# One weight tile cut by partitions, and w_ch moved behind it

## The chip, the cores and the metric
The kernel runs on one core of a Trainium2 chip. The metric is device time in microseconds (us): the median of several runs. Beside it there is one profiled execution, whose span (first to last instruction) and trace are read here. TensorE (PE) multiplies, VectorE (DVE) and ScalarE (ACT) work element by element, GpSimd (POOL) here mostly issues transfers, SyncE (SP) issues the stores and the first loads.

## The reference, cut to what matters
Attention with a forgetting decay, then a spectral mix of 64 Fourier modes along the sequence, then a residual channel product:

```python
# q, k, v: 8 x 8 heads x 576 x 64; f: 8 x 8 x 576
scores = q @ k.T / 8 + (cum[i] - cum[j])        # cum: running sum of log f; causal
x = softmax(scores) @ v                         # put together as 8 x 576 x 512
X = rfft(x, axis=1)[:, :64]                     # 64 modes of 512 channels
Yr = Xr @ w_r - Xi @ w_i                        # w_r, w_i: 64 x 512 x 512, one matrix a mode
Yi = Xr @ w_i + Xi @ w_r
u = x + irfft(Y)
out = u + relu(u @ w_ch)                        # w_ch: 512 x 512
```

The inputs are float32 in HBM; w_r and w_i are 67 MB each, and every weight is used once. w_ch is 1 MB.

## The kernel before
**Two stages.** The first runs over 32 pairs of heads (plus two iterations to drain): transposes of q and k, scores, exponentials, the product with v, and the Fourier sums of each finished pair. From its iteration 10 on, `spec_early` also multiplies the first channel blocks with their weights. The second stage runs over the 16 groups `u` of four modes and, in each, over the channel blocks `dc` still missing; between them `xw` and `fold` multiply by w_ch and bring the modes back to the sequence. After the last weight come 18 steps that add up and store the result.

**The weights.** `wseq` lists the weight tiles in the order of use: first the 28 of `early`, (u, 0) for 16 groups and (u, 1) for 12; then for each u what is left. A tile with `dc < 2` holds w_r and w_i of four modes for 128 channels and comes as two transfers (L156), which `issue_half` sends one at a time. A tile with `dc` 2 or 3 holds w_r or w_i of four modes for 256 channels, two channels on each partition, and comes as one transfer of 128 partitions (L165): 2 MB read from HBM as float32, 1 MB written as bfloat16. The first tile of that kind is number 28, `n == len(early)`; it is sent by the `issue_half` of iteration 29 of the first stage. The very last tile of `wseq` comes mode by mode in four transfers. Tiles lie in seven buffers of `wpool` and, for five of them, in memory that is not yet in use (`guests`).

**The queue.** All weights, q, k, and v but for its first three, are issued by GpSimd, in the order in which the program is written: in each iteration q and k of the pair four ahead (L109), half a tile, v of the pair three ahead (L119), another half (left out in iterations 3, 6, 9, 12 and 15). An issue waits until its buffer is free, and until the transfer eight before it on this queue is complete (eight semaphores are used in turn). The transfers convert float32 to bfloat16 on the way (v excepted).

**w_ch.** `setup_late`, called once in iteration 2, loads all of w_ch in one transfer of 128 partitions (L322): 1 MB read, 0.5 MB written. On each partition lie four rows, the blocks `eb` 0 to 3. Its first reader is `xw` (L694) in the second stage; `fold_modes` (L718) and `last_modes` (L893) read it later.

**The end.** For the last group, `spec_cols` (L211) takes the last tile mode by mode as its four transfers land; then `last_modes`, `rest`, `base` and the stores follow (L953).

Of the kernel before, what the change touches and what calls it, by code (L numbers as in the profile page):

```python
# [17 lines left out]
def _strided(ap: bass.AP, free_dims, offset_elems: int = 0) -> bass.AP:  # L18
    new_ap = [list(ap.ap[0])] + [list(x) for x in free_dims]
    return bass.AP(tensor=ap.tensor, offset=ap.offset + offset_elems, ap=new_ap)  # L20
# [3 lines left out]
def kernel(  # L24
# [11 lines left out]
    nc = tc.nc  # L36
# [32 lines left out]
    wch = const.tile([128, NEB, D], BF16, name="wch")  # L69
# [55 lines left out]
    early = [(u, 0) for u in range(NU)] + [(u, 1) for u in range(NX)]  # L125
# [14 lines left out]
    def issue_w(half=None):  # L140
        n = wissued[0]
        if n >= len(wseq):
            return
        u, dc = wseq[n]
        if half != 1:
            if n in guests:
                w8 = guests[n][:, 0 : 8 * D].rearrange("p (t m e) -> p t m e", t=2, m=4)
            else:
                shape = [128, 2, 4, D] if dc < 2 else [128, 4, 2, D]
                w8 = wpool.tile(shape, BF16, tag="w8", name="w8")  # L150
            wtile[(u, dc)] = w8
        w8 = wtile[(u, dc)]
        if dc < 2:
            for t, src in enumerate((moe_w_r, moe_w_i)):
                if half in (None, t):
                    nc.gpsimd.dma_start(  # L156
                        w8[:, t, :, :],
                        src[4 * u : 4 * u + 4, dc * 128 : (dc + 1) * 128, :].rearrange("m p e -> p m e"),
                    )
        elif half != 1:  # L160
            src = (moe_w_r, moe_w_i)[dc - 2]
            step = 1 if n + 1 == len(wseq) else 4
            for j in range(0, 4, step):
                m = 4 * u + j
                nc.gpsimd.dma_start(  # L165
                    w8[:, j : j + step, :, :].rearrange("p m r e -> p m (r e)"),
                    src[m : m + step, 256:512, :].rearrange("m (p r) e -> p m (r e)", r=2),
                )
        if half != 0:
            wissued[0] += 1  # L170

# [2 lines left out]
    def issue_half():  # L174
        issue_w(whalf[0])
        whalf[0] ^= 1
# [138 lines left out]
    def setup_late():  # L315
        nc.vector.memset(XS[:, :, 24 * NM : XROW], 0.0)
        nc.vector.tensor_copy(
            perm[:].rearrange("p (b j ri) -> p b j ri", b=8, j=4),
            ident_bf[:].rearrange("p (j x ri b) -> p b j x ri", j=4, x=2, ri=2)[:, :, :, 0, :],
        )  # L320
        nc.vector.tensor_copy(rep[:], _strided(ident_bf[:, KF:128], [[0, 4], [1, KL]]))
        nc.gpsimd.dma_start(wch[:], moe_w_ch.rearrange("(eb p) e -> p eb e", p=128))  # L322

    def setup_bi(sc):
        ns = SBLK[sc]
# [226 lines left out]
    for i in range(NPAIR + 2):  # L552
# [56 lines left out]
        if i == 2:  # L609
            setup_late()  # L610
# [12 lines left out]
    with ExitStack() as bctx:  # L623
# [44 lines left out]
        with ExitStack() as mctx:  # L668
# [97 lines left out]
            for u in range(NU):  # L766
# [4 lines left out]
                for dc in range(first, NEB):  # L771
# [37 lines left out]
                    else:  # L809
                        spec_mms(A, u, dc, dc == first, dc == NEB - 1)  # L810
                    issue_w()
                if last:
                    break
# [103 lines left out]
        for i in range(len(steps)):  # L917
# [11 lines left out]
            p, sb = steps[i][0]  # L929
# [54 lines left out]
```

## Time and profile before

| | |
|---|---|
| median of 3 runs | 436.59 us (436.33 to 437.64) |
| profiled execution | 436.43 us, span 434.6 us |
| busy: PE, DVE, ACT, POOL | 343.3, 267.9, 234.1, 145.0 us |
| read from HBM, written | 163.73 MB, 9.44 MB |
| GpSimd's transfers (q0) | 62800 packets, 85.64 MB |

Busy times are sums over an engine's instructions. Bytes of a queue are counted as written, so a weight counts half of what is read for it. "q8" and "q14" are the queues that carry instructions, q1 that of SyncE's loads and stores. A transfer is done in sixteen shares; the trace keeps the time at which each is complete. Rows of a timeline give start, duration, engine, line, operation and, in brackets, the idle time before and what ended it; rows of the chain that ended last give start, duration and what. All times count from the span's start.

### The profile page before, as it was taken

What the parts mean: (1) busy time and instruction counts of PE and PEld (TensorE: products, weight loads), DVE (VectorE), ACT (ScalarE), POOL (GpSimd) and SP (SyncE); (2) the same over time, 40 slices, a digit from 0 to 9 for tenths busy, and PEclk for the clock granted to TensorE, in tenths of its full rate; (3) what the DMA queues carried; (4) which work ended last, traced back from release to release, by engine and by line L of the source; (5) the groups of instructions that cost most, each with busy time, mean ns of one, the idle gap of its engine ahead of it and who ended that gap; (6) DMA issues with size and microseconds to landing.
All of it is one profiled execution on the core that took longest, in us unless ns stands there. A gap on an engine that the chain in (4) does not pass through costs nothing.

```text
span 434.6 us, 10304 instructions
## 1 busy us (share of the span) xinstructions
PE 343.3 (79%) x4264; PEld 189.6 (44%) x4274; DVE 267.9 (62%) x651; ACT 234.1 (54%) x358; POOL 145.0 (33%) x215
## 2 busy tenths in 40 slices
PE   1689787798898898988896386599877498888993
PEld 1455555554555565555553142244433233334330
DVE  6677888877778778888885122222233165565794
ACT  4556777687887766656660022024322166564783
POOL 6544445444544353444213211111122202110273
PEclk9986999999999999999999579589999699999998
DMA  8999999999999999999999999999999999998498
GB/s 185 205 233 220 233 219 232 225 227 233 231 229 227 226 228 225 228 225 228 227 218 213 212 212 211 212 212 213 211 212 212 209 209 211 210 209 158 168 383 323
DMA packets 68543, 96.76 MB, mean 223 GB/s; under 512 B 3728, under 2 KB 45200, under 8 KB 68496
## 3 DMA queue, kind: packets, MB, share of 16 engines
q0 software_dynamic: 62800, 85.64, 106.3%
q1 hardware_dynamic: 5696, 10.47, 6.6%
q8 instruction: 33, 0.54, 0.4%
q14 instruction: 14, 0.11, 0.1%
HBM read 163.73 MB, written 9.44 MB: 398 GB/s over the span
## 4 chain that ended last, share of the span: by engine, by line
DMA 43%; PE 31%; DVE 18%; issue 3%; ACT 3%; POOL 1%; DVEq 0%; POOLq 0%
DMA w<-in_moe_w_r_dram 22%; DMA w<-in_moe_w_i_dram 20%; PE pav L477 5%; DVE vT L384 4%; DVE qkT L360 4%; DVE x_all L492 4%; PE A L194 4%; PE sps L432 3%; PE tv L382 3%; PE pd L521 3%; PE vp L393 2%; DMA qk<-in_k_dram 2%; PE Z L654 2%; DVE vn L372 2%; PE U L654 2%
## 5 line engine op out<-in xcount | busy, mean ns | idle before, releaser
L439 ACT ACTIVATE et<-sps 128x1024 bf16<-128x1024 f32 x96 | 96.0, 1049 | 13.9 <-PE sps L432 11.5
L477 PE MATMUL pav<-vs,et 128*128 128x65 bf16 (+1 forms) x896 | 52.1, 198 | 0.2 <-DVE vn L372 0.2
L360 DVE COPY qkT<-tp 128x640 bf16<-128x640 bf16 x64 | 48.7, 763 | 2.8 <-PE tp L355 2.8
L815 DVE TENSOR_TENSOR Yb<-A,yx 128x512 bf16<-128x512 f32 x15 | 10.4, 691 | 61.0 <-PE A L194 60.9
L477 PEld LDWEIGHTS <-et 128*128 128x128 bf16 (+1 forms) x896 | 37.2, 103 | 17.9 <-issue 13.6
L432 PE MATMUL sps<-qkT 64*128 64x512 bf16 (+4 forms) x320 | 39.8, 312 | 1.1 <-DVE qkT L360 1.1
L194 PE MATMUL A<-w,XP 128*16 128x512 bf16 (+1 forms) x240 | 21.9, 449 | 23.0 <-DMA w<-in_moe_w_i_dram 12.8
L694 PE MATMUL pxw<-wch,xT 128*128 128x512 bf16 (+1 forms) x152 | 39.0, 402 | 0.9 <-issue 0.3
L492 DVE TENSOR_TENSOR x_all<-pav,rcp 128x384 bf16<-128x384 f32 (+2 forms) x96 | 36.2, 377 | 3.3
L355 PE MATMUL tp<-ident_bf,qk 128*64 128x128 bf16 x576 | 30.3, 237 | 9.3 <-DMA qk<-in_k_dram 9.3
L384 DVE COPY vT<-tv 128x576 bf16<-128x576 bf16 x32 | 24.2, 757 | 19.8 <-PE tv L382 19.8
L165 POOL DMA_DIRECT2D w<-in_moe_w_r_dram x16 | 11.9, 743 | 71.8 <-PE A L194 50.5
L701 ACT CAST XW<-pxw 128x512 bf16<-128x512 f32 (+1 forms) x16 | 9.4, 585 | 47.3 <-PE pxw L694 47.3
L156 POOL DMA_DIRECT2D w<-in_moe_w_r_dram x27 | 20.5, 758 | 38.7 <-DMA w<-in_moe_w_i_dram 9.4
L404 ACT COPY vs<-vp 128x576 bf16<-128x576 bf16 x32 | 20.5, 640 | 21.7 <-PE vp L400 21.7
L165 POOL DMA_DIRECT2D w<-in_moe_w_i_dram x19 | 13.3, 698 | 53.3 <-PE A L194 31.6
L701 ACT CAST yx<-pxw 128x512 bf16<-128x512 f32 (+1 forms) x24 | 14.0, 585 | 31.4 <-PE pxw L694 31.4
L109 POOL DMA_DIRECT2D qk<-in_q_dram x32 | 19.5, 610 | 32.5 <-PE sps L432 6.2
L741 ACT CAST x_all<-pu 128x512 bf16<-128x512 f32 (+1 forms) x40 | 23.4, 584 | 11.2 <-PE pu L740 10.3
L491 DVE RECIPROCAL rcp<-pav 128x6 f32<-128x6 f32 (+2 forms) x96 | 16.2, 169 | 17.4 <-PE pav L477 17.3
L156 POOL DMA_DIRECT2D w<-in_moe_w_i_dram x27 | 20.3, 752 | 18.4 <-DMA w<-in_moe_w_i_dram 8.2
L109 POOL DMA_DIRECT2D qk<-in_k_dram x32 | 19.2, 601 | 19.3 <-DMA w<-in_moe_w_i_dram 5.2
(149 smaller groups left out, 677.8 us busy)
## 6 DMA issues: line engine op xcount, KB each, us to landing
w<-in_moe_w_r_dram POOLq DMA_DIRECT2D x16, 1024.0 KB, 29.5
w<-in_moe_w_i_dram POOLq DMA_DIRECT2D x15, 1024.0 KB, 31.7
w<-in_moe_w_r_dram POOLq DMA_DIRECT2D x27, 512.0 KB, 11.1
w<-in_moe_w_i_dram POOLq DMA_DIRECT2D x27, 512.0 KB, 12.3
out_dram<-o_sb SPq DMA_DIRECT2D x36, 256.0 KB, 3.2
vt<-in_v_dram POOLq DMA_DIRECT2D x29, 288.0 KB, 10.7
qk<-in_q_dram POOLq DMA_DIRECT2D x32, 144.0 KB, 10.8
qk<-in_k_dram POOLq DMA_DIRECT2D x32, 144.0 KB, 10.4
```

The costliest lines, as they stand in the source:

```text
L109: nc.gpsimd.dma_start(qk[64 * n : 64 * n + 64, :, :], src[b, 2 * g : 2 * g + 2, :, :].rearrange("h (p r) d -> p h (r d)", p=64),)
L156: nc.gpsimd.dma_start(w8[:, t, :, :], src[4 * u : 4 * u + 4, dc * 128 : (dc + 1) * 128, :].rearrange("m p e -> p m e"),)
L165: nc.gpsimd.dma_start(w8[:, j : j + step, :, :].rearrange("p m r e -> p m (r e)"), src[m : m + step, 256:512, :].rearrange("m (p r) e -> p ...
L194: nc.tensor.matmul(A[32 * j : 32 * j + M, :], lhsT=lhsT, rhs=rhs, start=st_, stop=sp_)
L355: nc.tensor.transpose(tp[64 * hp : 64 * hp + 64, r - r0, :, :].rearrange("p n c -> p (n c)"), qk[:, hp, r * 64 : r * 64 + 64], ident_bf[:, :],
L360: nc.vector.tensor_copy(st[i]["T"][:].rearrange("p n (c r) -> p n c r", r=9)[:, :, :, r0:r1], tp[:, 0 : r1 - r0, :, :].rearrange("p r n c ...
L384: nc.vector.tensor_copy(st[i]["vT"][:].rearrange("p (c r) -> p c r", r=9), tv[:].rearrange("p r c -> p c r"))
L432: nc.tensor.matmul(ps[:, hp, c : c + n], lhsT=KT[sl, jb * 128 : jb * 128 + 128], rhs=QT[sl, i0 : i0 + n], start=True, stop=True,)
L439: nc.scalar.activation(st[i]["et"][:, T, :, :], ps[:], ACT.Exp, scale=scale)
L477: nc.tensor.matmul(pav[:Ms, sb % 3, hp, :], lhsT=eblk(i, hp, jb, sb), rhs=rhs, start=(jb == 0), stop=(jb == sb),)
L492: nc.vector.tensor_tensor(x_all[:ns, g, b, lo:hi, :].rearrange("p s (h d) -> p s h d", h=2), pav[:ns, lo % 3 : lo % 3 + n, :, 0:Dh], _stri ...
L694: nc.tensor.matmul(pxw[rows, :], lhsT=xT[:, eb, sb * 128 : sb * 128 + Ms], rhs=wch[:, eb, :], start=(eb == 0), stop=(eb == NEB - 1),)
```

## The change
The first tile of the second kind, number 28, is loaded in three transfers, of partitions 0 to 14, 15 to 63 and 64 to 127 (15, 49 and 64 of them), in place of one of 128. Right behind it, in the same `issue_w`, w_ch is loaded in three: its blocks 0 and 1 in partitions 0 to 71 and 72 to 127 (72 and 56), then its blocks 2 and 3 in all 128. The load in `setup_late` is gone.

```diff
             step = 1 if n + 1 == len(wseq) else 4
+            cuts = (0, 15, 64, 128) if n == len(early) else (0, 128)
             for j in range(0, 4, step):
                 m = 4 * u + j
-                nc.gpsimd.dma_start(
-                    w8[:, j : j + step, :, :].rearrange("p m r e -> p m (r e)"),
-                    src[m : m + step, 256:512, :].rearrange("m (p r) e -> p m (r e)", r=2),
-                )
+                rows = src[m : m + step, 256:512, :].rearrange("m (p r) e -> p m (r e)", r=2)
+                for p0, p1 in zip(cuts, cuts[1:]):
+                    nc.gpsimd.dma_start(
+                        w8[p0:p1, j : j + step, :, :].rearrange("p m r e -> p m (r e)"), rows[p0:p1]
+                    )
+            if n == len(early):
+                rows = moe_w_ch.rearrange("(eb p) e -> p eb e", p=128)
+                for p0, p1, e0 in ((0, 72, 0), (72, 128, 0), (0, 128, 2)):
+                    nc.gpsimd.dma_start(wch[p0:p1, e0 : e0 + 2, :], rows[p0:p1, e0 : e0 + 2, :])
...
         nc.vector.tensor_copy(rep[:], _strided(ident_bf[:, KF:128], [[0, 4], [1, KL]]))
-        nc.gpsimd.dma_start(wch[:], moe_w_ch.rearrange("(eb p) e -> p eb e", p=128))
```

Every byte that was loaded is still loaded once, on the same queue.

## The prediction

> **What bounds the kernel now.** I read the page first: the DMA row, the queues and the chain that ended last.
>
> ```profile
> span 434.6 us, 10304 instructions
> ...
> DMA  8999999999999999999999999999999999998498
> ...
> q0 software_dynamic: 62800, 85.64, 106.3%
> ...
> q8 instruction: 33, 0.54, 0.4%
> ...
> DMA 43%; PE 31%; DVE 18%; issue 3%; ACT 3%; POOL 1%; DVEq 0%; POOLq 0%
> ```
>
> The transfer engines are busy in every slice but the last few, and the transfers that GpSimd issues (q0) carry nearly all of it. Next, the chain in order of time, in the last 100 us, shows where the stream hands over to the tail:
>
> ```profile
> 352.85 29.27 DMA w<-in_moe_w_r_dram
> 382.12 0.28 issue
> 382.40 19.71 DMA w<-in_moe_w_i_dram
> 402.12 0.05 issue
> 402.16 0.41 PE AT L211 x8
> ...
> 428.65 0.60 DVE o_sb L938
> ```
>
> The last weight piece lands at 402.12. What follows is arithmetic and stores, 32.5 us to the end of the span, and none of it is touched. So the question is what moves 402.12.
>
> The trace keeps sixteen completion marks for each transfer, one for each transfer engine, without the engine's number. For the last piece, sorted, in us behind the first (396.61):
>
> ```
> 0.00 0.55 0.63 0.87 0.88 1.50 1.70 | 3.58 4.59 4.62 4.89 4.96 5.22 5.25 5.27 5.51
> ```
>
> Seven engines are early, nine late, and the kernel waits for the last. The offsets are not one transfer's accident: from 214 us to the end each 1 MB weight transfer passes all sixteen at the same 4.95 us pace (first marks at 217.73, 222.68, 227.64), and the offsets stay, apart from single steps of about 1.06 us on one engine at a time. The steps go with the packets of q8: 33 of 16 KB, each taking 0.89 to 1.03 us. The first starts at 23.35, and the transfer landing then has its last mark at 25.39, 1.06 behind the next to last (24.32), where the one before it had 0.03 there. Their durations repeat in turns of eight (949, 945, 935, 974 ns open the first turn, 949, 944, 935, 974 the fourth), so I read them as eight engines served in rotation. By 396 us 32 of them have run, four for each of eight engines: 4 x 1.06 = 4.24, plus the spread of 0 to 1.04 that all had at 18 us. That is the group at 4.59 to 5.51; the 3.58 is then an engine hit by the smaller fetches of q14. When an early engine has finished (396.61) the others do not speed up: the last four pieces still come 1.25 apart. Each engine has its own pace, so work taken off a late engine comes off the end, and work put on an early one costs nothing until it is the last.
>
> **The change part by part.** It moves no arithmetic: the instructions of TensorE, VectorE and ScalarE stand in the same order, so the q8 fetches stay 33.
>
> *w_ch out of the setup (L322).* Its half megabyte passed an engine in 2.54 us (first marks 41.21 and 43.75). Everything behind it on GpSimd's queue comes up to 2.54 us earlier until the tile that brings it back. The sum over the span is nothing as long as no engine runs dry: GpSimd's issues in the attention follow the completion of the transfer eight before (0.28 to 0.6 us after it nearly always), so the depth stays. Where buffers hold GpSimd instead (78.27 and 148.47, some 1.5 us late), the queue could lose 2.54 of a depth (issue to first mark) of 7.82 and 6.35, leaving 5.28 and 3.81; the very first transfer, into an empty queue, took 3.27. Covered, by 0.5 us at the worst. If that cover were gone it would cost the early engines alone, up to 2.5. w_ch's first reader is L694 at 252.0 us, and it now lands near 230: 20 us to spare.
>
> *One tile in three transfers, w_ch in three.* The tile is the first of L165; GpSimd's rows are
>
> ```profile
> 210.23 0.74 POOL L165 DMA_DIRECT2D w<-in_moe_w_r_dram  x1 [0.31 <-issue]
> 211.05 0.74 POOL L165 DMA_DIRECT2D w<-in_moe_w_i_dram  x1
> 217.54 0.74 POOL L165 DMA_DIRECT2D w<-in_moe_w_r_dram  x1 [5.75 <-PE tv L382]
> ```
>
> Six issues replace one here: five more at 0.55 to 0.74 us, 3.3 us of GpSimd, hidden by the 5.75 it idles. They also use up the eight places in flight: the next tile's issue (211.05) now waits for the mark that stood at 219.68, less 2.54, so about 217.2. Behind it wait only the further tiles; the early engines pass the tile ahead at 217.73 - 2.54 = 215.2 and then have 12 rows (7.4 us) and some 2 us of w_ch, the late ones start 3 us later with 5 rows and 3 us of w_ch: work until about 224. A transfer needs some 3 us, so it is covered by 4. Five more transfers cost each engine something: quarter tiles pass in 1.25 to 1.27 against 4.95 / 4 = 1.24, so 0.02 each, 0.10 in all.
> [...]
>
> *Who carries the rows.* 64 and 128 partitions cost all sixteen engines alike. No row of before shows 15, 49, 72 or 56. A row of the tile costs an engine 4.95 / 8 = 0.62 us, a row of half of w_ch 2.54 / 16 = 0.16. Bounds: spread evenly, nothing changes; given to few engines, some gain rows and others lose them. I take equal shares over the largest number of engines up to sixteen that divides the count, because a transfer in equal shares is what every row shows: 15 as 15x1, 49 as 7x7, 64 as 16x4, 72 as 12x6, 56 as 14x4, each going on where the one before stopped. Counting engines from where the 15 starts as 0: the 49 lies on 15 and 0 to 5, the 72 on 6 to 15, 0 and 1, the 56 on 2 to 15. (15+7+12+14 is 48, so the turn closes.) Against 8 rows each:
> - 0 and 1: tile 1+7+4 = 12, w_ch 6: +4 x 0.62 - 2 x 0.16 = +2.16
> - 2 to 5: 12 and 4: +2.48 - 0.64 = +1.84
> - 15: 0+7+4 = 11 and 10: +1.86 + 0.32 = +2.17
> - 6 to 14: 1+4 = 5 and 10: -1.86 + 0.32 = -1.54
>
> Seven engines get more, nine less, and the trace has seven early and nine late. If these are the same, the late end at 5.51 - 1.54 = 3.97 and the early at most at 1.70 + 2.17 = 3.87: the gap closes almost exactly. That fit of numbers and of sizes is why I take this placement, though no row names an engine.
> [...]
>
> *Sum.* -1.54 + 0.10 = -1.44 us on 402.12. TensorE must follow:
>
> ```profile
> 341.88 1.06 PE L194 MATMUL A<-w,XP 128*16 128x512 bf16 x8 [4.25 <-DMA w<-in_moe_w_i_dram]
> 371.86 0.64 PE L194 MATMUL A<-w,XP 128*16 128x512 bf16 x8 [0.81 <-DMA w<-in_moe_w_i_dram]
> 402.16 0.40 PE L211 MATMUL AT<-XP,w 128*128 128x16 bf16 x8 [0.31 <-DMA w<-in_moe_w_i_dram]
> ```
>
> It waits 4.25 us for a tile at 341.88, so its work from there starts 1.44 earlier too, and the later, small waits move with it. Span 434.6 - 1.44 = 433.16; the profiled execution's 436.43 lies 1.83 above its span, which gives 434.99. The median of the runs shown, 436.59, is 0.16 above that execution: 435.15, say 435.1.
>
> **The rivals.**
> 1. *The seven heavy shares meet late engines* (slower). Decided by where the turn stands: one engine of the 4.59 to 5.51 group among the heavy seven is enough. It ends at up to 5.51 + 2.17 = 7.68 instead of 5.51: 436.59 + 2.17 + 0.10 = 438.9. For it: the trace names no engine. Against it: seven and nine match, and so do the prices. Chance 0.15.
> 2. *Shares rounded up over sixteen*: 15 as one each on fifteen, 49 as four on twelve and one on a thirteenth, 72 as five, 56 as four. Twelve engines then carry 9 and 9 rows: +0.62 + 0.16 = 0.78; four lose. With nine late engines, at least five of the twelve are late: 4.96 to 5.51 + 0.78 + 0.10, so +0.3 to +0.9, 436.9 to 437.5. [...] Chance 0.12.
> 3. *TensorE does not follow.* Between 341.88 and 402.16 its waits for weights are 0.3 to 0.8 each, and it ran at half clock near 340 to 350 (0.43 us a matmul against 0.22). If that stretch does not move with the landings, only the last waits are won: 0.3 to 0.8, so 435.8 to 436.3. Chance 0.05.
> 4. *Nothing uneven happens* (the transfers spread over all sixteen whatever their count): +0.1, 436.7. Chance 0.04.
>
> The forecast keeps 0.64.
>
> **How the numbers follow.** 0.3% is 1.31 us, about what a measurement of this kernel can tell from no change. The forecast's 1.44 is just over it, so of its 0.64 I give 0.56 to faster and 0.08 to falling short of the bound. Same: that 0.08 with rivals 2, 3 and 4 (0.12, 0.05, 0.04), 0.29. Slower: rival 1, 0.15. The best that any division could do is level all sixteen at their mean, 3.13, which saves 2.38: 434.2; with the scatter of the runs, 434.0 is the low end. The high end, 437.5, takes in rival 2 and leaves out rival 1.
>
> **What would show it.** In the profile after, the sixteen marks of the last piece should lie within 4 us, with last near 400.7 and the first near 398.5, and the marks of the 49-partition transfer should bunch: seven engines busy 4.3 us, nine passing at once. w_ch's first reader should wait for nothing, and GpSimd's issue of the next tile should stand near 217. Wrong would be: a last mark over 403 with a spread of 7 (rival 1), a spread near 6 (rival 2), or an earlier landing with an unmoved end (rival 3).

## The result: 438.02 us, slower by a quarter of a per cent

The changed kernel takes 438.02 us (22 runs, 437.13 to 439.64), the kernel before 437.0 in the same comparison (22 runs, 436.02 to 438.0): ratio 1.0026, 95% interval 1.0016 to 1.0035. That is 1.1 us by the ratio and 1.0 by the medians, inside the 0.3% that the prediction took as its bound but clear over 22 runs of each. It is on the other side of no change from the forecast (435.1), and past the high end of its range (437.5). The profiled execution took 437.98 us.

The page of the changed kernel, in the rows shown of before, has the same stream and a span 1.6 us longer:

```profile
span 436.2 us, 10319 instructions
...
DMA  8999999999999999999999999999999999997498
...
q0 software_dynamic: 63184, 85.64, 106.3%
...
q8 instruction: 33, 0.54, 0.5%
...
DMA 42%; PE 34%; DVE 17%; ACT 3%; issue 3%; POOL 1%; DVEq 0%; POOLq 0%; ACTq 0%
```

The bytes are the same to the last figure, the instruction fetches (q8) are 33 as before. The sixteen marks of the last piece, in us behind the first (395.75; before 396.61), are

```
0.00 0.32 3.48 3.72 3.75 4.14 4.67 4.86 4.88 4.94 4.97 5.07 5.42 5.79 6.96 8.20
```

The first engine is done 0.86 earlier than before and the last 1.83 later, at 403.95 instead of 402.12. Before, seven engines were early and nine late. Now two are far ahead, two far behind, and the rest lie together. TensorE's rows at the same three places (start, duration, engine, line, and the idle time before with what ended it) are

```profile
342.91 1.06 PE L200 MATMUL A<-w,XP 128*16 128x512 bf16 x8 [4.21 <-DMA w<-in_moe_w_i_dram]
372.88 1.06 PE L200 MATMUL A<-w,XP 128*16 128x512 bf16 x8 [1.84 <-DMA w<-in_moe_w_i_dram]
404.00 0.40 PE L217 MATMUL AT<-XP,w 128*128 128x16 bf16 x8
```

The three stand 1.03, 1.02 and 1.84 later than before. The last has no wait behind it: TensorE gets there 0.05 after the last mark, so stream and TensorE end together in this run. The chain that ended last accordingly runs over the weights to 372.84 and then over TensorE:

```profile
309.24 33.63 DMA w<-in_moe_w_i_dram
342.91 0.49 issue
343.40 29.44 DMA w<-in_moe_w_i_dram
...
404.00 0.42 PE AT L217 x8
...
430.48 0.60 DVE o_sb L943
```

The clock granted to TensorE in that stretch was 0.89 where it was 1.00 before. The windows (busy time of PE, PEld, DVE, ACT, POOL with instruction counts, then granted clock, DMA share and GB/s) of before and then after:

```profile
372.00:402.00 30.00, 26.23 (x226) 11.84 (x221) 16.69 (x28) 15.94 (x28) 3.35 (x8) 1.00 1.05 192
```

```profile
372.00:402.00 30.00, 26.57 (x204) 11.86 (x203) 15.99 (x27) 15.53 (x28) 3.34 (x8) 0.89 1.07 194
```

In eight of the eleven profiled runs compared in the next sections (all but those of the probes), the time is the last mark plus 34.0 to 34.5 us (before 436.43 - 402.12 = 34.31, after 34.03). In the other three (e1_move, e2_cut, e10_fit) it is 35.2 to 35.4, and there TensorE reached the last piece 1.1 to 1.2 us after the mark, with 0.89 granted in the same window in all three. So the last mark sets the time, and in these three single runs the low clock went with some 1 us more; in the changed kernel, with the same 0.89, the late mark covers it (34.03). A last mark by itself scatters: that of e1_move stands at 403.15, 1.03 behind that of before, with no uneven share in it and with timed runs that agree with those of before. So a last mark is read below together with the pattern of the sixteen and with the timed runs.

GpSimd's rows after show the issues in their new order:

```profile
207.70 1.34 POOL L168 DMA_DIRECT2D w<-in_moe_w_r_dram  x2 [0.44 <-PE s L428]
210.46 0.62 POOL L168 DMA_DIRECT2D w<-in_moe_w_r_dram  x1 [1.42 <-DMA w<-in_moe_w_r_dram]
211.21 0.68 POOL L174 DMA_DIRECT2D wch<-in_moe_w_ch_dram  x1
213.73 0.63 POOL L174 DMA_DIRECT2D wch<-in_moe_w_ch_dram  x1 [1.84 <-DMA w<-in_moe_w_i_dram]
216.31 0.71 POOL L174 DMA_DIRECT2D wch<-in_moe_w_ch_dram  x1 [1.96 <-DMA w<-in_moe_w_r_dram]
217.86 0.76 POOL L168 DMA_DIRECT2D w<-in_moe_w_i_dram  x1 [0.83 <-PE sps L437]
```

Pieces of 15 and 49 go out together, then the 64, then w_ch in three, and the next tile at 217.86. The marks of the 49-partition piece, behind its first at 215.84, show the cut at work:

```
0.00 0.07 2.49 4.08 4.17 4.18 4.31 4.38 4.47 4.54 4.98 5.08 5.09 6.50 8.15 8.64
```

### The profile page after: what moved, and what is told of

Same layout as the page of the kernel before. It is cut to its first block, busy times and chain, and to the rows that moved or that the text cites. A ratio compares the mean times of both kernels' runs of the same rounds, so it can differ in the third digit from the quotient of the medians.

```text
span 436.2 us, 10319 instructions
## 1 busy us (share of the span) xinstructions
PE 347.5 (80%) x4274; PEld 191.2 (44%) x4274; DVE 268.3 (61%) x651; ACT 234.1 (54%) x358; POOL 147.5 (34%) x219
## 4 chain that ended last, share of the span: by engine, by line
DMA 42%; PE 34%; DVE 17%; ACT 3%; issue 3%; POOL 1%; DVEq 0%; POOLq 0%; ACTq 0%
DMA w<-in_moe_w_i_dram 28%; DMA w<-in_moe_w_r_dram 12%; PE pav L482 5%; DVE vT L389 4%; DVE x_all L497 4%; DVE qkT L365 4%; PE A L200 4%; PE sps L437 3%; PE tv L387 3%; PE vp L398 2%; PE pd L526 2%; DMA qk<-in_k_dram 2%; PE Z L659 2%; PE U L659 2%; DVE vn L377 2%
## 5 line engine op out<-in xcount | busy, mean ns | idle before, releaser
L168 POOL DMA_DIRECT2D w<-in_moe_w_r_dram x18 | 13.1, 727 | 68.7 <-PE A L200 36.9
L156 POOL DMA_DIRECT2D w<-in_moe_w_r_dram x27 | 20.5, 759 | 41.7 <-PE A L200 8.8
L689 DVE COPY xT<-ptr 128x576 bf16<-128x576 bf16 x32 | 14.6, 457 | 19.2 <-PE ptr L684 18.3
```

The source lines that it names most:

```text
L156: nc.gpsimd.dma_start(w8[:, t, :, :], src[4 * u : 4 * u + 4, dc * 128 : (dc + 1) * 128, :].rearrange("m p e -> p m e"),)
L168: nc.gpsimd.dma_start(w8[p0:p1, j : j + step, :, :].rearrange("p m r e -> p m (r e)"), rows[p0:p1])
```

## Experiments

**The theories.** A: the division is as forecast (equal shares over the largest divisor, in turn), but the heavy shares fall on engines of the late group. B: the heavy engines are the early ones, and the loss comes from elsewhere: from w_ch's new place, from five more transfers, or from a queue that runs empty. C: the division itself is another. The first three kernels do one part of the change each.

**e1_move: w_ch moved, nothing cut.** The tile is whole, w_ch comes whole behind it.

```diff
-            cuts = (0, 15, 64, 128) if n == len(early) else (0, 128)
+            cuts = (0, 128)
-                for p0, p1, e0 in ((0, 72, 0), (72, 128, 0), (0, 128, 2)):
-                    nc.gpsimd.dma_start(wch[p0:p1, e0 : e0 + 2, :], rows[p0:p1, e0 : e0 + 2, :])
+                nc.gpsimd.dma_start(wch[:], rows)
```

Expected:

> w_ch comes in one transfer of 128 partitions behind tile 28, which stays whole. Theory P (placement: the loss of 1.0 us comes from heavy shares that meet late engines): no uneven share is left, so equal to the kernel before within 0.3 us, last piece complete with the same spread of about 5.5 us. Theory M (the move itself lets an engine run dry or comes too late): the 1.0 us stays. Theory C (every added transfer costs): one transfer as before, so no change.

Measured: 436.92 against 436.97, ratio 0.9994 (0.9978 to 1.001); the last piece's marks run from 397.04 over 6.11 us, to 403.15, with seven early and nine late, as before. The move costs nothing that the timed runs can tell; the last mark of this one execution is the late one named above.

**e2_cut: the tile cut in 15, 49 and 64, w_ch left in the setup.**

```diff
+            cuts = (0, 15, 64, 128) if n == len(early) else (0, 128)
...
+                for p0, p1 in zip(cuts, cuts[1:]):
```

Expected:

> The tile in 15, 49 and 64 partitions, w_ch whole in the setup as before. Theory P: the seven heavy shares stay (+4 or +3 rows of 0.62 us), so slower by 0.7 to 2.5 us, and the sixteen marks of the last piece spread over about 8 us. Theory M: equal to before. Theory C: two transfers more, +0.2 us at most, with a spread of 5.5 us.

Measured: 438.47 against 436.97, ratio 1.0032 (1.0017 to 1.0046). The last piece's marks, behind 394.99:

```
0.00 0.88 4.13 4.22 4.34 4.48 4.54 4.69 4.97 5.08 5.39 5.40 5.72 6.45 6.86 8.62
```

The pattern of the changed kernel is there with the cut of the tile alone: two ahead, one alone at the end, last mark 403.61. The cut is what costs.

**e3_even: as many transfers, but in even shares.** 16, 48 and 64 partitions, and w_ch in 64, 64 and 128.

```diff
-            cuts = (0, 15, 64, 128) if n == len(early) else (0, 128)
+            cuts = (0, 16, 64, 128) if n == len(early) else (0, 128)
-                for p0, p1, e0 in ((0, 72, 0), (72, 128, 0), (0, 128, 2)):
+                for p0, p1, e0 in ((0, 64, 0), (64, 128, 0), (0, 128, 2)):
```

Expected:

> As many transfers in the same places as in the changed kernel, but in 16, 48 and 64 partitions, and w_ch in 64, 64 and 128: all of these divide evenly over sixteen engines. Theory P: equal to before within 0.3 us, spread 5.5 us. Theory C (five more transfers cost each engine 0.1 to 0.5 us): slower by 0.1 to 0.5 us with the spread of before. Theory M: slower by about 1 us.

Measured: 437.39 against 436.97, ratio 1.001 (0.9993 to 1.0027); last mark 402.25, 0.13 from before. From the tile ahead of the cut to the tile behind w_ch an average engine needs 12.63 us, in e1_move 12.56: the added transfers cost an engine 0.07. The interval alone (up to 0.27%) would leave room for the loss of the changed kernel, but the marks keep the pattern of before, seven early and nine late over 5.65 us, where those of e2_cut, with fewer transfers, do not. So the count of transfers is not the cause; the unevenness is.

**e4_probe: which engine is which?** Eight transfers of two rows from one place in HBM to another (in `out`, ahead of its stores), one behind every second large tile.

> The kernel before with eight more transfers of two rows (16 KB read each) in the second stage, one behind every second weight tile; they put other rows into a part of out that is stored later. A look at the sixteen marks: if a transfer of two partitions goes to two neighbouring engines and the next one goes on behind them (the division in equal shares with a turning start), each probe delays two of the sixteen marks by 0.6 us or more, and the eight together each pair once, so that the late and the early engines can be told by their place in the turn. If the late nine are neighbours in the turn, the first theory of placement stands; if late and early alternate, no block of seven fits.

A miss: 438.02 in one run (before 436.97), and no mark stepped away from the others, so they told no engine from another.

**e5_probe17: sixteen transfers of 17 partitions x 512 into a tile.** 17 is a prime, so by the forecast's division one engine would take all of it.

```diff
+                nc.gpsimd.dma_start(
+                    XS[17 * r : 17 * r + 17, 0, 512 * c : 512 * c + 512],
+                    moe_w_r[0, 256:290, :].rearrange("(p r) e -> p r e", r=2)[:, 0, :],
+                )
```

> The kernel before with sixteen more transfers of 17 partitions (2 KB read on each, into memory that is no longer in use), one behind each of sixteen successive weight tiles of the second stage. 17 has no divisor up to sixteen but 1. Theory P (equal shares over a divisor, the next transfer going on behind the last): each one falls on a single engine and delays one of the sixteen marks by 17 x 0.08 = 1.3 us, and the sixteen together go once round the engines, so the order in which late and early marks move is the order of the engines in the turn. With the placement that the prediction took, counted from the turn's start, the marks of 0 to 5 and 15 are early ones and those of 6 to 14 late ones; if late engines lie among 15 and 0 to 5, that is the error. Rounded-up shares: nine marks move by 0.16 us each time.

439.16 in one run (before 436.13). No engine took all. Nine marks, the same nine each time, fell behind by 0.16 (eight of them) or 0.07 (one) with each probe; the seven others kept their pace. By these times that is a share rounded up, two rows on eight engines (0.16), one on a ninth (0.07), none on seven, and it starts at the same engine each time. Numbered from there, and as the next probe numbers them, the two rows lie on engines 0 to 7 and the one on 8. Of engines 0 to 7 five marks are early, one lies in the middle and two are late; engine 8 is early; of 9 to 15 one is early and six are late. So the early seven are not one run of neighbours, as the forecast had them. In this two-dimensional form, then, 17 partitions were divided as rival 2 had it.

**e6_probe17x2: the same with a third dimension.** Two blocks of 256 in place of one of 512, the shape of a weight tile.

```diff
-                    XS[17 * r : 17 * r + 17, 0, 512 * c : 512 * c + 512],
-                    moe_w_r[0, 256:290, :].rearrange("(p r) e -> p r e", r=2)[:, 0, :],
+                    XS[17 * r : 17 * r + 17, 0, 512 * c : 512 * c + 512].rearrange("p (m e) -> p m e", m=2),
+                    moe_w_r[0:2, 256:273, 0:256].rearrange("m p e -> p m e"),
```

> The same sixteen small transfers of 17 partitions, but each partition's 2 KB now in two pieces from two matrices (17 x 2 x 256 elements), a shape in three dimensions as the tile's (49 x 4 x 1024) and w_ch's (72 x 2 x 512) are; in two dimensions (17 x 512) the shares were rounded up over nine engines, always the same nine. If three dimensions are shared by a divisor from a turning start, each transfer now delays one mark by 1.3 us, a different one each time, and the marks of heavy and light engines in the changed kernel follow from that order. If three dimensions are rounded up as well, nine marks move 0.16 each time, and the changed kernel's 1.0 us must come from twelve engines with one row more.

442.14 in one run (before 436.86). Now each probe holds up a single mark by 1.22 us, another one each time, and after sixteen each has had its turn. The marks of the tile ahead of the first probe (behind 267.13), of the first and of the second probe (behind 267.31 and 272.48):

```
0.00 0.21 0.32 0.34 0.78 1.12 1.36 2.58 3.15 3.25 3.39 4.00 4.77 5.74 5.81 5.95
0.00 0.25 0.34 0.82 1.17 1.38 1.56 2.61 3.15 3.29 3.41 3.99 4.78 5.75 5.82 5.94
0.00 0.23 0.33 0.81 1.36 1.54 2.37 2.60 3.15 3.28 3.40 3.98 4.77 5.74 5.80 5.93
```

At the first one of the marks near 0.34 goes to 1.56: engine 0. At the second 1.13 goes to 2.37: engine 1. Followed through all sixteen, and read at the last piece, where every engine has had one probe, the lags are

```
engine  8    7    15   0    4    1    2    3    9    5    6    14   13   11   12   10
lag   0.00 0.22 0.32 0.34 0.80 1.15 1.71 3.11 4.25 4.35 4.47 5.11 5.75 5.87 5.95 6.89
```

(15 and 0 are a pair that can't be told apart by 0.02.) The early seven are 0, 1, 2, 4, 7, 8 and 15; 3 lies between; 5, 6 and 9 to 14 are late. The heavy seven of the cut, 15 and 0 to 5, hold five early engines, the middle one and a late one, number 5; the early engines 7 and 8 were relieved instead. Theory A holds. The division by the largest divisor in turn, which the forecast took, agrees with these rows: 17 partitions held up one mark by 1.22 us at each probe, and sixteen probes sixteen different ones.

**The order as a lever: four kernels in two pairs.** If the engines are known, the same pieces should help or hurt by their order alone. e7_fit and e8_misfit cut w_ch (behind the whole tile) by 51, 60 and 17 partitions in different order; e10_fit and e11_misfit cut a quarter of the tile (w_ch in the setup) by 69, 36 and 23.

```diff
# e7_fit, against e1_move                      (e8_misfit: 0, 60, 77, 128)
-                nc.gpsimd.dma_start(wch[:], rows)
+                cuts = (0, 51, 111, 128)
+                for p0, p1 in zip(cuts, cuts[1:]):
+                    nc.gpsimd.dma_start(wch[p0:p1, :, :], rows[p0:p1])
```

> The tile whole, w_ch behind it in 51, 60 and 17 partitions (rows of 8 KB read, 0.32 us each). By the order of engines that the probe gave, 51 = 3 x 17 falls on 0, 1 and 2, 60 = 12 x 5 on 3 to 14, 17 = 1 x 17 on 15: the early engines 0, 1, 2 and 15 get 9 rows more (+2.9 us, to 4.4 at most), the eight late ones and engine 3 three fewer (-0.95). Placement theory: the last piece is complete 0.8 to 0.9 us earlier, so some 436.1 against 437.0, with a spread under 5 us. If only the number of transfers or the cutting counts: 437.0 to 437.2, as for the next kernel.

> The same three pieces in another order: 60, 17 and 51 partitions. Now 60 falls on engines 0 to 11, 17 on 12 and 51 on 13, 14 and 15: three late engines get 9 rows more. Placement theory: the last of them ends 2.9 us later, so some 439.9, with a spread over 8 us. If only the number of transfers counts: the same time as in the other order.

Measured: e7_fit 440.55 against 437.0, ratio 1.0077 (1.0059 to 1.0095); e8_misfit 437.58, ratio 1.0012 (0.9996 to 1.0029). The names came out the wrong way round, because the expectation divided 60 over fewer engines than it could. 60 divides by 15. In e7_fit the 51 gives 17 rows each to engines 0, 1, 2, the 60 gives 4 each to all but engine 2, and the 17 falls on engine 2 whole: 34 rows on one engine, where 8 are even. Its marks say so: one at 10.16, 3.5 behind the next. In e8_misfit the 60 takes 0 to 14, the 17 engine 15 and the 51 engines 0, 1, 2: all four heavy ones are early, and the last mark stands at 402.76. The same three pieces, by order alone, are 3.0 us apart by the medians. TensorE's row for the last piece in e7_fit and in e8_misfit:

```profile
406.97 0.41 PE L218 MATMUL AT<-XP,w 128*128 128x16 bf16 x8 [0.31 <-DMA w<-in_moe_w_i_dram]
```

```profile
402.80 0.41 PE L218 MATMUL AT<-XP,w 128*128 128x16 bf16 x8 [0.31 <-DMA w<-in_moe_w_i_dram]
```

In both it waits for the landing. By its shares e8_misfit should have gained, since its late engines carry four rows fewer (1.27 us); it did not, and what it lost is taken up under "The size".

**e9_fit_setup: e7_fit's pieces in the setup.**

```diff
-        nc.gpsimd.dma_start(wch[:], moe_w_ch.rearrange("(eb p) e -> p eb e", p=128))
+        rows = moe_w_ch.rearrange("(eb p) e -> p eb e", p=128)
+        cuts = (0, 51, 111, 128)
+        for p0, p1 in zip(cuts, cuts[1:]):
+            nc.gpsimd.dma_start(wch[p0:p1, :, :], rows[p0:p1])
```

> The good order (51, 60, 17), but in the setup, where the kernel before loads w_ch; no move. Placement theory: an engine keeps what it has lost or won to the end, so the place does not matter: the same 0.8 to 0.9 us as with the move, unless the queue, which is only some 10 us deep there, runs dry for the engines with 5 rows (then 0.3 to 0.9 less won).

Measured: 441.88, ratio 1.0116 (1.0091 to 1.014). Here something else is lost. At the last tile ahead of the large ones the average engine is 6.4 us late (226.63 against 220.20), and from there on it keeps the pace of before (10.07 against 10.06 for two tiles). GpSimd's rows show one place:

```profile
45.21 0.60 POOL L109 DMA_DIRECT2D qk<-in_q_dram  x1 [3.27 <-PE sps L435]
47.99 0.60 POOL L109 DMA_DIRECT2D qk<-in_k_dram  x1 [2.17 <-DMA wch<-in_moe_w_ch_dram]
49.02 0.76 POOL L156 DMA_DIRECT2D w<-in_moe_w_r_dram  x1 [0.43 <-DMA wch<-in_moe_w_ch_dram]
```

The issue waits for the heaviest engine's mark on a piece of w_ch, eight transfers back, while other engines run out of work. In the windows of before and then of this kernel, the stream moves 168 GB/s at 48 to 52 us in place of 231:

```profile
48.00:52.00 4.00, 3.71 (x70) 2.33 (x71) 3.59 (x12) 3.47 (x5) 1.57 (x4) 1.00 1.20 231
```

```profile
48.00:52.00 4.00, 3.51 (x68) 2.25 (x68) 3.63 (x11) 3.65 (x4) 1.35 (x2) 1.00 1.08 168
```

Uneven shares close to the front, where the queue is not yet deep, made the whole stream late here. How much of the 6.4 us this is was not separated: from 60 to 76 us the clock granted to TensorE was 0.50 in this execution and 1.00 before.

**e10_fit and e11_misfit: a quarter of the tile.**

```diff
+                for p0, p1 in ((0, 69), (69, 105), (105, 128)):   # e11_misfit: (92, 128), (69, 92), (0, 69)
+                    nc.gpsimd.dma_start(w8[p0:p1, 2:4, 0, :], rows[p0:p1, 2:4, 0, :])
```

> w_ch as in the kernel before. A quarter of tile 28 (the first channel of each partition, for two of its four modes; a row of it costs 0.15 us) in 69, 36 and 23 partitions, the rest in two even transfers. With the largest divisor up to sixteen counted rightly (in the runs before, 60 divides by 15, not only by 12, so their 17 and 51 fell on other engines than written there): 69 = 3 x 23 on engines 0, 1, 2, 36 = 12 x 3 on 3 to 14, 23 on 15. The early engines 0, 1, 2, 15 get 15 rows more (+2.2 us, to some 4), all eight late ones five fewer (-0.75). Placement theory, with the 0.1 us that the uneven pieces of the tile alone cost an engine on average: last piece 0.4 to 0.7 us earlier, 436.3 to 436.6 against 437.0, spread 4.5 to 5. If uneven pieces cost by themselves, as w_ch's seem to: 437.0 or above.

> The same five transfers, the three pieces in the order 36, 23, 69: 36 on engines 0 to 11, 23 on 12, 69 on 13, 14 and 15. Three late engines (12, 13, 14) get 2.2 us more. Placement theory: 438.8 to 439.4, spread 7 to 8 us, some 2.5 us above the other order. If placement is nothing: the same as the other order.

69 is 3 x 23, 36 is 12 x 3, 23 a prime. In e10_fit engines 0, 1, 2 and 15 are heavy (23 rows of the quarter where 8 are even), in e11_misfit 12 to 15. Measured: e10_fit 437.0 against 437.31, ratio 0.9988 (0.9977 to 0.9999); e11_misfit 440.68, ratio 1.0063 (1.0039 to 1.0086). Order alone is worth 3.7 us by the medians, and the sign is as the engines' numbers say. In e11_misfit the last three marks stand at 6.43, 7.03 and 8.80 behind 398.60, and TensorE waits for them:

```profile
407.45 0.40 PE L220 MATMUL AT<-XP,w 128*128 128x16 bf16 x8 [0.31 <-DMA w<-in_moe_w_i_dram]
```

e10_fit's spread is 5.72, no narrower than before. Its profiled run is the highest of its thirteen (440.75), and its stream was late ahead of the cut (221.95 against 220.20), so its last mark says little. At best this division gains 0.23%; none of the kernels beats the one before by more.

**e12_wch_cut: the other half of the change.** The tile whole, w_ch in 72, 56 and 128 behind it.

```diff
-            cuts = (0, 15, 64, 128) if n == len(early) else (0, 128)
+            cuts = (0, 128) if n == len(early) else (0, 128)
```

> The changed kernel with the tile whole: only w_ch is moved and cut in 72, 56 and 128. By shares: 72 gives engines 0 to 11 six rows, 56 gives 12 to 15 and 0 to 9 four, so 0 to 9 have 10 rows of 0.16, 10 and 11 have 6, 12 to 15 four: +0.32, -0.32, -0.64. Placement alone: +0.1 to +0.3 by engines 5, 6 and 9. In the changed kernel the engines lost 0.8 us on average over the place of the change beyond the rows they got, and with the tile alone 0.1. If w_ch's pieces are what costs it, this one shows that loss too: 437.5 to 438.0. If the loss needs both cuts: 437.1 to 437.3.

Measured: 437.65 against 437.31, ratio 1.0013 (0.9995 to 1.0031), last mark 402.91, spread 5.79. From the tile ahead to the tile behind an average engine needs 12.63, as in e3_even. By itself this cut costs nothing that can be told.

## Why the prediction was wrong, step by step

**What bounds the kernel: right.** Every kernel here, but for the three with the low clock named above, has its time by the last mark, and from the second large tile to the last piece an average engine needs 169.4 to 169.5 us in all eleven kernels without probes, whatever the cut. Each engine does have its own pace, and rows put on one stay on it to the end: the lone mark of e7_fit, made by the rows of w_ch behind tile 28, is still 3.5 us behind the next at the last piece.

**The move: right, with less cover than forecast.** e1_move shows it free. GpSimd's issue of the next tile stands at 217.86, forecast near 217, and w_ch's first reader waits for nothing:

```profile
252.69 3.60 PE L699 MATMUL pxw<-wch,xT 128*128 128x512 bf16 x8
```

But the cover of 4 us was worked out for early engines with heavy shares and late ones with light shares. Engines 7 and 8 are early and light: by the trace's packets they are through with w_ch at 220.8 and 221.0, and by the forecast's own "some 3 us" for a transfer next to nothing of the cover was left. It was enough: the next tile begins on them at once, 2.95 us after its issue. Their packets show no gap, and the windows of e3_even and then of the changed kernel agree: two idle engines of sixteen would leave 189 of the 216 GB/s (the last figure), and there are 206.

```profile
221.20:222.20 1.00, 1.00 (x14) 0.32 (x11) 1.00 (x4) 0.47 (x1) 0.74 (x1) 1.00 1.21 216
```

```profile
221.20:222.20 1.00, 0.79 (x17) 0.64 (x17) 0.66 (x2) 0.32 (x2) 0.43 (x1) 1.00 1.19 206
```

**The division: right.** No row of before had shown it; the runs do. Heavy marks of the 49 move on by 4.33, seven rows of 0.62, against nine that pass; e6 shows the turning start by itself (1.22 us on another mark each time), and the lone mark of e7 (3.5 us behind the next) and the two pairs by order (3.0 us between e7 and e8, 3.7 between e10 and e11) agree with it. The profile's pages count it too. Of before, of the changed kernel and of e6_probe17x2:

```profile
DMA packets 68543, 96.76 MB, mean 223 GB/s; under 512 B 3728, under 2 KB 45200, under 8 KB 68496
```

```profile
DMA packets 68927, 96.76 MB, mean 222 GB/s; under 512 B 4112, under 2 KB 45584, under 8 KB 68880
```

```profile
DMA packets 77503, 97.07 MB, mean 220 GB/s; under 512 B 12144, under 2 KB 54160, under 8 KB 77456
```

The changed kernel has 384 packets more for the same bytes, all of them small (4 bytes each in the trace). Before, 3088 packets of 4 bytes are on q0, sixteen for each of its 193 transfers, as many as there are completion marks. Sixteen for each of the four added transfers make 64, and e3_even has just these 64. The other 320 come out if each engine gets as many packets as the heaviest one, with small packets in place of the rows that it lacks. A row of the tile is four packets (of 2 KB in the trace) and a row of half of w_ch two (of 1 KB), so 15 as 15x1 adds 4, 49 as 7x7 adds 9 x 28 = 252, 72 as 12x6 adds 4 x 12 = 48 and 56 as 14x4 adds 2 x 8 = 16. Shares rounded up (rival 2) would add 96.

**Who carries the rows: wrong, and this is the step that failed.** The forecast gave the heavy shares to 15 and 0 to 5 and took these for the early seven, because seven and nine matched and the prices too, "though no row names an engine". It was two claims, and only the first was right. The second was a coincidence of counts. It is rival 1, which had 0.15 and needed one late engine among the heavy: that engine is number 5. With e6's lags the forecast's own prices give the marks again: engine 5 at 4.35 + 1.84 = 6.19, engine 3 at 3.11 + 1.84 = 4.95, engine 8 at -1.54, a spread of 7.73; measured 8.20. For e2_cut (12 rows against 5, so +2.48 and -1.86) they give a last mark of 396.61 + 4.35 + 2.48 = 403.44 and a first of 394.75; measured 403.61 and 394.99.

**The size.** Rival 1's 438.9 took the very last engine with the largest share (5.51 + 2.17). The late engine in question lies at 4.35 and gets 1.84, which brings the last mark only 0.68 past that of before. Measured are 1.83 in the profiled execution and 1.0 to 1.1 in the timed runs. Since a last mark scatters by 1 us (e1_move), the difference cannot be divided to the tenth. One part of it is a term that the forecast set at 0.10 for "five more transfers": an average engine of the changed kernel needs 13.38 us from the tile ahead to the tile behind w_ch, against 12.63 in e3_even with as many transfers, so 0.75 more.

It comes with uneven pieces only. The three pieces of the tile take an average engine 0.77 + 2.16 + 3.02 = 5.95 in the changed kernel, 0.65 + 1.81 + 2.50 = 4.96 in e3_even. The small packets are one cause. Each probe of e6 held up the fifteen engines that got no row by 0.2 us, with 34 small packets on each, so one costs some 6 ns (an estimate from these two numbers). The tile's 256 are then 0.1 us on the average of sixteen engines, which is all that e2_cut loses (10.17 against 10.06). The other 0.6 us lie at 222 to 226 us, where the packets of the changed kernel take longer. The windows of e3_even and then of the changed kernel (the last two figures are DMA share and GB/s):

```profile
222.00:226.00 4.00, 3.97 (x75) 2.61 (x71) 3.45 (x10) 3.60 (x6) 0.86 (x2) 1.00 1.18 209
```

```profile
222.00:226.00 4.00, 4.00 (x72) 2.30 (x72) 3.17 (x9) 2.74 (x4) 1.25 (x2) 1.00 1.35 172
```

The engines are busy there and slower: 172 GB/s in place of 209 is 0.7 us in 4. e2_cut and e12_wch_cut, with one cut each, move 206 and 207 GB/s there. What slows the packets stays open, and so does whether every timed run has it.

The small packets may also be why no order gained; this is worked out, and no run tests it alone. e8_misfit has 1920 of them, some 0.7 us on the average engine; it loses 0.96 (13.53 us from tile to tile, e1_move 12.57). Its late engines are relieved of 1.27 us of rows and get 136 small packets, some 0.8 us by the same estimate. In e10_fit they are relieved of 0.75 and get 92, some 0.55.

**TensorE follows: right in the main.** The landing moved by 1.83 and the profiled execution by 1.55. The medians are only 1.0 apart, because the profiled execution of before (436.43) was faster than its median (437.0) while that of after was not; how much of that is clock and how much landing was not separated.

**What was to show it.** The prediction named "a last mark over 403 with a spread of 7" as the sign of rival 1. The marks are at 403.95 and 8.20; the spread is the part that tells, since e1_move has a last mark of 403.15 with a spread of 6.11.

## What to carry to other kernels

This stream was bound by the slowest of sixteen engines, and the same uneven shares came out 3.0 us (e7_fit and e8_misfit) and 3.7 us (e10_fit and e11_misfit) apart by their order alone. So first find out which engine is which: here a small transfer that landed on one engine, sent in turn, named them by the mark that it delayed (e6_probe17x2, 1.22 us). A match of counts ("seven heavy, seven early") is no identification. Work out the divisor of each piece anew (60 divides by 15 as well as by 12, and e7_fit came out with one engine 3.5 us behind the next), count what an uneven piece costs the engines that it leaves out (0.2 us a probe in e6_probe17x2), and look twice at uneven pieces where the queue is shallow: with them in the setup the stream of e9_fit_setup came 6.4 us late, at a low clock for part of it.

## What the runs showed of the hardware that was not expected

- The same 17 partitions are divided in two ways by their form: 17 x 512 rounded up over engines 0 to 8 (e5_probe17: 0.16 and 0.07 us a probe), 17 x 2 x 256 whole on one engine, another each time (e6_probe17x2: 1.22 us). With two rows from HBM to HBM (e4_probe) no mark stepped away from the others.
- By e7_fit's times the turn seems to start anew with each launch: its pieces (3 + 15 + 1 = 19 shares) would leave the turn three engines on, and yet its six runs lie within 439.89 to 441.16, where the other order of the pieces takes 437.58.
- The packet counts come out if an engine that gets fewer rows of a transfer than the heaviest one gets packets of 4 bytes in their place: 320 of them in the changed kernel. In e6_probe17x2 an engine without a row gets 34 and loses 0.2 us (a tile with its probe in 5.15 us in place of 4.95). In e5_probe17 it gets two and loses 0.02. The packets of both pages fit: sixteen probes add 8960, which is 16 x (34 for the rows + 16 marks + 15 x 34), and 768, which is 16 x (17 + 16 + 15).
- The eight late engines are 5, 6 and 9 to 14: at the last piece of e6_probe17x2 they stand 4.25 to 6.89 us behind engine 8, the seven early ones 0 to 1.71. In before 32 instruction packets of 16 KB have started by 396.02 us, and the mark that steps back with the first of them does so by 1.06 us; four such steps on each of eight engines would be 4.24 us, an estimate from these numbers.
